# A recurrent attention with decay and a two-layer feed-forward: v*s as pieces of the output's column groups, two more stages with tiles from ScalarE and DMA transposes, and q~/k~ formed behind two sums

## The chip, the cores and the metric

The kernel runs on one core of one Trainium2 chip. The metric is the time of one execution on the device in microseconds; a kernel's time is the median of several runs. TensorE (PE) multiplies matrices from SBUF into PSUM, VectorE (DVE) and ScalarE (ACT) work elementwise, GpSimd (POOL) issues the loads and forms some tiles, and SyncE (SP) issues the stores and the DMA transposes.

## The reference

Two parts follow each other. The first is a linear attention with a decayed state, for 4 batches and 8 heads, 768 tokens of 48 channels:

```python
for t in range(S):
    cur = einsum('bhd,bhe->bhde', u[None] * k[t], v[t])
    y[t] = einsum('bhd,bhde->bhe', r[t], state + cur)
    state = w[None, :, :, None] * state + einsum('bhd,bhe->bhde', k[t], v[t])
```

The second takes y as 3072 rows of 384 channels: `h = x @ w_in` (384 to 2048), `g = max(0.01 h, h)`, `out = g @ w_out` (2048 to 384). Inputs and output are float32.

## The kernel before

**Stages.** The tokens are cut into 24 stages of 128 (6 for each batch, n = 0 to 23). Inside a stage the recurrence is written as matrix products: with q~ = r times a power of w and k~ = k times a power of w, a stage needs the products A = k~ q~ for each head, masked to the strict triangle; a state `st` carried from stage to stage; and the diagonal, whose entry s = sum over channels of r u k multiplies v. The output of a stage comes out transposed, channels on partitions, which is what the first product of the feed-forward takes as its moving operand.

**Steps of a stage**, with the letters that the written order uses: P (`prep`) forms q~ and k~ on DVE; T (`turn`) transposes them, eight TensorE matmuls against the identity and two evictions by ACT; A (`a_mm`) is the products into PSUM, M (`a_mask`) writes them masked to the tile `at` on DVE; X (`diag`) forms q~ times k~ on DVE for the diagonal; K (`kv_mm`) is k~ times v for the state, and S (`state`) decays it on DVE; Q (`prep2`) forms what the diagonal needs; Y (`y_part`) sums everything into the output and ACT copies it to `xT`.

**Two ways for the diagonal.** For stages below `DIAG` = 8, s comes out of TensorE as extra columns in K's bank (four matmuls against `wu`), Q forms `vs` = v*s on DVE, and Y ends with three whole 128x128 matmuls of `vs` against the identity. From stage 8 on, Q computes s on DVE (`ku`, `rku`, `s_tok`) and a tile of ident*s is laid into `at` ahead of the mask, which is then a predicated copy that leaves the diagonal: by POOL for stages 8 to 13 (two instructions for each stage), by ACT for later ones (eight for each stage). For stages below `TURNED` = 8, T transposes on TensorE; from 8 on, P forms q~ and k~ in one DVE instruction and SP issues one DMA transpose from `qk` to `tp`.

**Column groups.** Y writes 32 output channels at a time, in four column groups of the array that work side by side; each group gets its pieces (A's halves, and the state's) in rounds of four matmuls.

**Feed-forward.** G (`g1`) is the first product for one stage and four blocks of 128, J (`g1_pair`) that for two stages and two blocks; ACT applies the activation. H (`g2`) is the second product of a stage (16 matmuls of 128x384) and a copy and a store. For pairs 5 to 11 (`SEVEN`) the second product is done in seven half-size products instead of eight (`g2_seven`), with sums of operands on DVE (`g_sum`, `w_sum`) and sums of results, `plus`, on DVE.

**Order.** Every engine runs its instructions in the order in which the program records them; waits are set from reads and writes of named keys, and a read of a key that nobody has written yet sets no wait. The first stages and the feed-forward of the first three pairs are written out by hand in `ORDER`; L8 to L13 in it are the loads of stages 8 to 13, and the first loads are in `LOADS`, in their order. From pair m = 3 on a loop records, for each pair: the eight J products, the s of coming stages, sums, loads, A and M of stages 2m+4 and 2m+5, Y of 2m+2 and 2m+3, K and S, P of 2m+6 and 2m+7, and then the second product of pair m - 1. PSUM has eight banks, taken in rotation; at the end of each pair banks are skipped so that the rotation starts at the same place.

**Queues.** All loads of r, k, v and the weights are issued by POOL, in order; stores and DMA transposes by SP, in order. `w_out` comes as four slices, recorded from 3 down to 0, behind the loads of stages 1 to 7 and `w_in`.

## Time and profile before

| | before |
|---|---|
| median of 3 runs | 169.2 us (168.89 to 169.73) |
| profiled execution | 168.76 us, span 167.0 us, TensorE clock 1.0 throughout |
| PE busy | 160.9 us (96% of the span), 2275 matmuls |
| DVE busy | 120.7 us (72%) |
| ACT busy | 116.2 us (70%) |
| POOL busy | 82.2 us (49%) |
| DMA | 19.68 MB; DMA transposes of tp: 16, median 4.7 us from issue to landing |
| loads by POOL | r, k, v: 96 KB each, 4.9 to 5.5 us in the median; w_out: four of 384 KB, 10.4 us |
| mean duration of one | J matmul (128x256) 273 ns, H matmul (128x384) 326 ns, Y piece (32 columns) 224 ns, T matmul 254 ns; ACT tile of ident*s 388 ns; POOL half tile 1140 ns; predicated copy 1220 ns |

The span is the time from the first to the last instruction of the profiled execution; what the run takes on top of it, 1.76 us, is outside the trace. Matmuls are pipelined, so the duration of one is longer than the distance to the next: what a group costs TensorE is read from start to start. Rows by time give the start and duration in us, the engine, the line, the operation, the tiles and, in brackets, idle time ahead of it and what ended it.

### The profile page before, as it was taken

The numbers are of one execution on the slowest core, as the hardware profiler recorded it, in microseconds if no ns is written. First come the engines' busy times: TensorE is split into PE (matmuls) and PEld (weight loads), VectorE is DVE, ScalarE is ACT, GpSimd is POOL, SyncE is SP. The second block draws the span as 40 slices with busy tenths as digits, with TensorE's granted clock in tenths as the row PEclk, the third lists the DMA queues.
The fourth block names the chain that finished last, engine by engine and source line by source line (L and its number), as shares of the span: only waits on it lengthen the run. The fifth ranks groups of instructions, "written<-read, shape, count | busy, mean of one in ns | idle before, by whom it ended". The sixth has DMA issues, their size and how long they took to land.

```text
span 167.0 us, 5346 instructions
## 1 busy us (share of the span) xinstructions
PE 160.9 (96%) x2275; PEld 133.1 (80%) x2275; DVE 120.7 (72%) x232; ACT 116.2 (70%) x262; POOL 82.2 (49%) x97
## 2 busy tenths in 40 slices
PE   6799999999999999999999999999999999999994
PEld 1568898889656876876876889899897898898993
DVE  7699848751998959999279998799798267046253
ACT  4753898789112861989989889989899836828530
POOL 7999999991379797894840830910000000000000
PEclk9999999999999999999999999999999999999999
DMA  5999999999999989979997996999407102002022
GB/s 99 117 157 155 170 152 173 200 190 144 137 150 207 152 72 108 190 87 121 144 193 85 194 109 98 191 81 97 126 4 167 53 4 98 0 4 94 0 96 96
DMA packets 99260, 19.68 MB, mean 118 GB/s; under 512 B 92323, under 2 KB 99237, under 8 KB 99237
## 3 DMA queue, kind: packets, MB, share of 16 engines
q0 software_dynamic: 76512, 10.03, 92.5%
q1 hardware_dynamic: 21682, 9.11, 27.6%
q8 instruction: 18, 0.29, 0.7%
q10 hardware_dynamic: 1042, 0.20, 0.6%
q14 instruction: 6, 0.04, 0.1%
HBM read 20.45 MB, written 4.72 MB: 151 GB/s over the span
## 4 chain that ended last, share of the span: by engine, by line
PE 89%; POOL 4%; DVE 3%; ACT 1%; issue 1%; POOLq 0%
PE ps_all L566 31%; PE ps_all L647 18%; PE ps_all L583 16%; PE ps_all L549 7%; PE ps_all L516 5%; PE ps_all L399 4%; PE ps_all L375 3%; PE ps_all L433 2%; POOL rk_sb L218 2%; DVE at L409 1%; PE ps_all L521 1%; ACT tp L386 1%; DVE sum_t L486 1%; POOL v_sb L218 1%; DVE out_sb L678 1%
## 5 line engine op out<-in xcount | busy, mean ns | idle before, releaser
L566 PE MATMUL ps_all<-xT,w_in_sb 128*128 128x256 bf16 x480 | 54.5, 273 | 0.0
L566 PEld LDWEIGHTS ps_all<-xT,w_in_sb 128*128 128x128 bf16 x480 | 46.7, 98 | 5.8
L572 ACT ACTIVATE gT<-ps_all 128x512 bf16<-128x512 f32 x80 | 47.0, 596 | 4.9 <-PE ps_all L566 1.2
L218 POOL DMA_DIRECT2D rk_sb<-in_k_dram x23 | 21.5, 934 | 16.4 <-PE ps_all L566 16.4
L409 DVE CAST_PREDICATED at<-mask,ps_all 128x1024 bf16<-128x1024 uint16 x16 | 18.8, 1220 | 11.8 <-PE ps_all L399 11.7
L583 PE MATMUL ps_all<-w_out_sb,gT 128*128 128x384 bf16 x160 | 27.2, 326 | 0.0
L363 ACT ACTIVATE at<-ident,s_tok 128x128 bf16<-128x128 bf16 x80 | 24.8, 388 | 0.0
L583 PEld LDWEIGHTS ps_all<-w_out_sb,gT 128*128 128x128 bf16 x160 | 15.3, 98 | 9.7
L218 POOL DMA_DIRECT2D v_sb<-in_v_dram x24 | 22.5, 945 | 0.4 <-issue 0.4
L218 POOL DMA_DIRECT2D rk_sb<-in_r_dram x23 | 21.4, 930 | 0.0
L357 POOL TENSOR_TENSOR at<-ident,s_tok 128x512 bf16<-128x512 bf16 x12 | 13.4, 1140 | 9.7 <-DVE s_tok L347 9.7
L678 DVE TENSOR_TENSOR out_sb<-ps_all,snap 128x192 f32<-128x192 f32 x22 | 7.5, 356 | 12.9 <-PE ps_all L647 12.1
L647 PE MATMUL ps_all<-tw,gs 128*128 128x192 bf16 x168 | 16.0, 246 | 0.0
L589 ACT ACTIVATE out_sb<-ps_all 128x384 f32<-128x384 f32 x10 | 4.9, 487 | 14.6 <-PE ps_all L583 14.6
L536 ACT ACTIVATE xT<-ps_all 128x384 bf16<-128x384 f32 x24 | 11.0, 491 | 4.8 <-PE ps_all L516 3.0
L647 PEld LDWEIGHTS ps_all<-tw,gs 128*128 128x128 bf16 x168 | 14.0, 98 | 0.0
L549 PE MATMUL ps_all<-xT,w_in_sb 128*128 128x128 bf16 x192 | 12.8, 224 | 0.0
L549 PEld LDWEIGHTS ps_all<-xT,w_in_sb 128*128 128x128 bf16 x192 | 11.7, 101 | 0.5 <-DMA w_in_sb<-in_moe_w_in_dram 0.2
L554 ACT ACTIVATE gT<-ps_all 128x512 bf16<-128x512 f32 x16 | 9.6, 598 | 3.6 <-PE ps_all L549 2.9
L647 PE MATMUL ps_all<-w_out_sb,gT 128*128 128x192 bf16 x112 | 11.6, 246 | 0.2 <-ACT xT L536 0.2
L621 DVE TENSOR_TENSOR gs<-gT 128x1024 bf16<-128x1024 bf16 x14 | 9.6, 685 | 2.9 <-ACT gT L572 2.9
L417 DVE TENSOR_TENSOR at<-ps_all,mask 128x512 bf16<-128x512 f32 x16 | 10.3, 683 | 1.2 <-PE ps_all L399 1.2
(81 smaller groups left out, 234.1 us busy)
## 6 DMA issues: line engine op xcount, KB each, us to landing
out_dram<-out_sb SPq DMA_DIRECT2D x22, 192.0 KB, 3.1
v_sb<-in_v_dram POOLq DMA_DIRECT2D x24, 96.0 KB, 5.5
rk_sb<-in_r_dram POOLq DMA_DIRECT2D x23, 96.0 KB, 5.3
rk_sb<-in_k_dram POOLq DMA_DIRECT2D x23, 96.0 KB, 4.9
w_in_sb<-in_moe_w_in_dram POOLq DMA_DIRECT2D x4, 384.0 KB, 7.5
w_out_sb<-in_moe_w_out_dram POOLq DMA_DIRECT2D x4, 384.0 KB, 10.4
out_dram<-out_sb SPq DMA_DIRECT2D x4, 96.0 KB, 1.6
tp<-qk SPq DMA_TRANSPOSE x16, 4.7
```

The costliest lines, as they stand in the source:

```text
L218: add("pool", lambda: G.dma_start(dst, src), R=pace, W=[key], dma=f"{which}{n}")
L357: add("pool", lambda hh=hh, s_of=s_of: G.tensor_tensor(at[ia][:, hh, :, :], ident[:, :].unsqueeze(1).to_broadcast([128, NP, 128]), s_of.un ...
L363: add("act", lambda h=h: A.activation(at[ia][:, h % 2, h // 2, :], ident[:, :], AF.Copy, scale=s_tok[n % 2][:, h:h + 1]), R=["ident", ("s" ...
L409: add("dve", lambda: V.copy_predicated(at[n % NAT][:, :, :, :].rearrange("p two m i -> p (two m) i"), mask[:, :].bitcast(mybir.dt.uint16). ...
L417: add("dve", lambda hh=hh, part=part: V.tensor_tensor(at[n % NAT][:, hh, :, :], part, mask[:, :].unsqueeze(1).to_broadcast([128, NP, 128]) ...
L536: add("act", lambda: A.activation(xT[m % NX][:, :, 128 * half:128 * half + 128], ps_y[:, 0:HD].rearrange("p (s t) -> p s t", t=128), AF.Copy),
L549: last = PE.matmul(ps_g[:, 128 * f:128 * f + 128], w_in_sb[:, s, 128 * fb:128 * fb + 128], xT[ix][:, s, t], start=s == 0, stop=s == NSL - 1)
L554: add("act", lambda: A.activation(gT[ig][:, 4 * grp:4 * grp + 4, t], ps_g[:, :].rearrange("p (f t) -> p f t", t=128), AF.Prelu, alpha=0.01 ...
L566: last = PE.matmul(ps_g[:, 256 * f:256 * f + 256], w_in_sb[:, s, 128 * fb:128 * fb + 128], xT[ix][:, s, :], start=s == 0, stop=s == NSL - 1)
L572: add("act", lambda: A.activation(gT[ig][:, 2 * j:2 * j + 2, :].rearrange("p f t -> p (f t)"), ps_g[:, :], AF.Prelu, alpha=0.01), R=[key], ...
L583: last = PE.matmul(ps_o[:, 0:HD], gT[ig][:, s, 128 * half:128 * half + 128], w_out_sb[:, s, :], start=s == 0, stop=s == NFB - 1)
L647: done = PE.matmul(ps_o[:, 0:NH], lhs[:, s, :], rhs[:, s, :], start=first and s == 0, stop=s == HF - 1, skip_group_check=not (first and last))
```

## The change

- **v*s as pieces.** For stages that still use `vs`, Y no longer ends with three whole matmuls. Each 32-column block gets one more piece, `vs` against the identity, inside its column group, and each block starts and stops its own sum.
- **Stages 6 and 7.** `TURNED` and `DIAG` go from 8 to 6: stages 6 and 7 are transposed by DMA (two more DMA transposes, T6 and T7 are gone), their s is formed on DVE, their state adds on DVE, and their masks are predicated copies. Which stages POOL makes tiles for is now `POOLED` = 8 to 13, so the tiles of 6 and 7 are made by ACT, at the new step D. `ORDER` is rewritten from P5 on: A6, A7, M6 and M7 stand behind H1, A8, A9, M8 and M9 behind H3, and P9, Q9, P10 behind M7.
- **A pace for P.** `prep` takes a second argument, which adds a read of the key ("pace", 4, behind); `ORDER` uses it once, as P6.6.
- **q~/k~ ahead behind two sums.** In pairs whose second product is done in seven, P of the coming stages (18 to 23) is recorded inside `g2_seven`, behind the first two `plus`, and no longer ahead of it.
- **Banks.** The skip of banks at the end of a pair is left out for m = 10 as well, since no stages are ahead there.

```diff
-T4 Q3 G2.0 G2.1 G0.2 S3 G2.2 G1.2 Y3 P5 A4 P6 X4 M4 T5 X5 G3.0 K4 Q4 A5 S4 T6 G3.1 K5 G3.2 Y4 M5 L8 Q5 Y5 P7 A6 G1.3 J2.0 J2.1 T7
-M6 X6 X7 K6 J2.2 J2.3 A7 S6 J2.4 J2.5 L9 Q6 G2.3 G0.3 J2.6 M7 L10 J2.7 L11 G3.3 K7 S7 P8 Q7 Q8 P9 H0 Q9 K8 H1 P10 L12 K9 H2 S8 S9
-Y6 Y7 A8 A9 P11 M8 H3 M9 L13
+T4 Q3 G2.0 G2.1 G0.2 S3 G2.2 G1.2 Y3 P5 A4 X4 M4 T5 X5 G3.0 K4 Q4 A5 S4 G3.1 K5 G3.2 Y4 M5 L8 Q5 Y5 G1.3 J2.0 J2.1 J2.2 J2.3 J2.4
+J2.5 L9 Q6 P6.6 P7 G2.3 G0.3 J2.6 L10 J2.7 L11 G3.3 K6 S6 K7 S7 Q7 D6 D7 P8 Q8 H0 H1 A6 A7 M6 M7 P9 K8 Q9 P10 L12 H2 K9 S8 S9
+Y6 Y7 P11 H3 A8 A9 M8 M9 L13
...
-    TURNED, DIAG = 8, 8
-    LED = 14
+    TURNED, DIAG = 6, 6
+    POOLED = range(8, 14)
...
-    def prep(n):
+    def prep(n, behind=None):
         iq = n % NQK
+        pace = [] if behind is None else [("pace", 4, behind)]
...
-                R=[("r", n % NRK), ("k", n % NRK), "qtab", "ktab", ("qk0", iq)], W=[("qp", iq), ("kp", iq)])
+                R=[("r", n % NRK), ("k", n % NRK), "qtab", "ktab", ("qk0", iq)] + pace, W=[("qp", iq), ("kp", iq)])
...
-            if whole:
+            if whole and n in POOLED:
                 diag_tile(n)
...
+                if n < DIAG:
+                    one.append((vs[iv][:, 128 * s + 32 * q:128 * s + 32 * q + 32], ident[:, :]))
                 todo += [(s, a, m, i == 0, i == len(one) - 1) for i, (a, m) in enumerate(one)]
...
-                                         start=first_mm and (s == 0 or n >= DIAG),
-                                         stop=last_mm and n >= DIAG)
-            if n < DIAG:
-                for s in range(NSL):
-                    last = PE.matmul(ps_y[:, 128 * s:128 * s + 128], vs[iv][:, 128 * s:128 * s + 128], ident[:, :],
-                                     start=False, stop=s == NSL - 1)
+                                         start=first_mm, stop=last_mm)
...
             plus(2, 0, 0, 0)
             product(0, 2, 2, False, False)
             plus(0, 1, 1, 1)
+            for n in behind:
+                prep(n)
             product(1, 3, (low, two), False, True)
             plus(1, 2, 0, 1)
...
-        for n in (2 * m + 6, 2 * m + 7):
-            if n < NST:
+        coming = [n for n in (2 * m + 6, 2 * m + 7) if n < NST]
+        if m - 1 not in SEVEN:
+            for n in coming:
                 prep(n)
...
-        if m < NST // 2 - 1:
+        if ahead:
             while taken[0] % 8 != y_first:
                 taken[0] += 1
...
-            second(m - 1, tiles=[(n, h) for n in further for h in range(H)])
+            second(m - 1, tiles=[(n, h) for n in further for h in range(H)], behind=coming)
```

More of the change, by code (lines that the diff above doesn't have):

```diff
@@ L353, in diag_tile @@
         ia = n % NAT
-        if n < LED:
+        if n in POOLED:
             for hh in range(2):
@@ L621, in g_sum, with g2_seven @@
         add("dve", lambda: V.tensor_tensor(x[i][:, :, :], a, b, op), R=keys, W=[("gs", m % 2, i)])
-    def g2_seven(m, early=(), late=(), tiles=()):
+    def g2_seven(m, early=(), late=(), tiles=(), behind=()):
         ig, i2 = m % NG, m % 2
@@ L736, in u_table @@
         add("act", lambda: A.activation(u_tab[:, :], ps_u[:, 0:HD], AF.Copy), R=[key], W=["u_tab"])
-    steps = {"U": u_table, "P": prep, "Q": prep2, "T": turn, "A": a_mm, "M": a_mask, "K": kv_mm, "S": state, "Y": y_part, "X": diag, "C": decay_columns, "W": decay_table, "F": fill,
+    steps = {"U": u_table, "P": prep, "D": diag_tile, "Q": prep2, "T": turn, "A": a_mm, "M": a_mask, "K": kv_mm, "S": state, "Y": y_part, "X": diag, "C": decay_columns, "W": decay_table, "F": fill,
              "G": g1, "J": g1_pair, "H": g2, "L": lambda n: load_stage(n, pace=[("pace", (n - 4) // 2, (n - 4) % 2)])}
@@ L741, in bass_rwkv5_eagle__then__act_leaky_relu_kernel, with second @@
         steps[name[0]](*(int(x) for x in name[1:].split(".") if x))
-    def second(m, early=(), late=(), tiles=()):
+    def second(m, early=(), late=(), tiles=(), behind=()):
         if m in SEVEN:
-            g2_seven(m, early, late, tiles)
+            g2_seven(m, early, late, tiles, behind)
         else:
@@ L752, in bass_rwkv5_eagle__then__act_leaky_relu_kernel @@
         ahead = [n for n in (2 * m + 4, 2 * m + 5) if n < NST]
-        further = [n for n in (2 * m + 6, 2 * m + 7) if LED <= n < NST]
+        further = [n for n in (2 * m + 6, 2 * m + 7) if n not in POOLED and n < NST]
         for j in range(8):
@@ L756, in bass_rwkv5_eagle__then__act_leaky_relu_kernel @@
         for n in ahead:
-            if n < LED:
+            if n in POOLED:
                 prep2(n)
```

## The prediction

> **What bounds the kernel now.** I read the page first, then the answers by time (PE, DVE, SP, POOL), then the landings of single transfers. The page:

> ```profile
> PE 160.9 (96%) x2275; PEld 133.1 (80%) x2275; DVE 120.7 (72%) x232; ACT 116.2 (70%) x262; POOL 82.2 (49%) x97
> DMA  5999999999999989979997996999407102002022
> PE 89%; POOL 4%; DVE 3%; ACT 1%; issue 1%; POOLq 0%
> ```

> TensorE is busy 96% of the span, so every matmul removed is worth its time unless something else is late there. DMA row: the engines are full until about 75 us, and the change puts new transfers into that stretch. So I read the stretch row by row (start, duration, ...):

> ```profile
> 41.52 2.76 PE L583 MATMUL ps_all<-w_out_sb,gT 128*128 128x384 bf16 x16
> 42.84 4.08 SPq L318 DMA_TRANSPOSE tp<-qk  x2
> 60.15 2.35 DVE L409 CAST_PREDICATED at<-mask,ps_all 128x1024 bf16<-128x1024 uint16 x2 [1.78 <-PE ps_all L399]
> 76.82 1.02 DVE L316 TENSOR_TENSOR qk<-rk_sb,tab 128x768 bf16<-128x768 bf16 x2
> 77.40 4.03 SPq L318 DMA_TRANSPOSE tp<-qk  x2
> 84.25 0.67 PE L399 MATMUL ps_all<-tp 48*128 48x128 bf16 x16
> ```

> H0 (first GEMM-2 product) starts at 41.52. DVE runs without a gap from M10 at 60.15 to P14/P15 at 76.82. The transposes of 14 and 15 follow at once, the second from about 78.7. How long it takes is in the issues of 78.70 to 78.75 us:

> ```profile
> tp<-qk SPq DMA_TRANSPOSE x1, 5.7
> ```

> 78.7 + 5.7 = 84.4, and A14/A15 start at 84.25: A15's operand is there 0.1 us before it is used (its 16 matmuls take 0.67 where the same group elsewhere takes 0.62). The chain of waits shows PE here, but DVE and the transposes stand just as close to the end. In the first 85 us PE time saved is worth something only if that chain moves too.

> **The change, part by part.**

> *PE work removed ahead of H0.* Start to start in the PE rows: T6 0.46, T7 0.45; the two s columns of K6 and K7 0.10 each; the carried state of K7 0.17: 1.28 us. A6 and A7 (0.33 each) only move behind H1. *Pieces:* a round of four column-group matmuls starts every 0.057 us (15.54, 15.60, 15.66, ...). Three more rounds are 0.17; the three whole matmuls they replace take 0.18 from start to start, so each of Y0 to Y5 gains 0 to 0.08, together 0.1. [...] *A part of T6 is lost:* Y5 needs v*s of stage 5, which DVE forms at 30.16 to 30.71, and DVE is late there for reasons that stay. PE would reach Y5 at 30.35 and waits to 30.7. So H0 is reached at 41.52 - 1.28 - 0.66 - 0.1 + 0.35 = 39.8.

> *New transposes of stages 6 and 7.* On DVE q~/k~ of 6 follow s of 6 (0.39 + 0.39 + 0.47, from 30.7) and end at 32.4; SP issues at 32.5. The token P6.6 should pace it, but the order listing of the changed kernel shows no wait at that row, because J2.6 is recorded later; instead J2.6 waits for P6, five microseconds early, which costs nothing. So both transposes enter while the output weights are landing. Weight slice 0, the last, is issued at 27.0:

> ```profile
> w_out_sb<-in_moe_w_out_dram POOLq DMA_DIRECT2D x2, 384.0 KB, 11.6
> ```

> This is the median of slices 1 and 0 (11.0 and 12.2): slice 0 lands at 39.2, 2.3 us before H0 now, and 0.6 us before the H0 of the changed kernel. What do two transposes cost the loads beside them? Alone, 2112 packets (two transposes) pass in about 2.5 us (125 to 131 us). Beside loads, the trace shows it once: from 44.3 on about 1.45 transposes are served until stage 11's v lands at 49.4, where the 0.7 us spacing of its neighbours puts it at 47.6: 1.8 us late for 1.8 us of service, one for one. Bounds for slice 0: 0 (room left) and 2.5 us (both served first); I take 2.3, near the upper end, since the pair of 42.84 was through within 8.2 us, which is 40.7 for a pair issued at 32.5. So H0 starts at 41.5, as now, and the 1.7 us won are gone. [...]

> *Behind H0* (A6 at t = H0 + 5.2 = 46.7). M6 starts at t+0.5, M6 and M7 take 2.3, so P9, now behind them, ends at t+3.3. K9 reads it: PE is there at 0.55 + 0.17 + 2.6 = t+3.3, no wait, but nothing spare. Behind K9 stand Y6, Y7 and H3, which need no more than M7. Y6/Y7 without their whole matmuls save 0.64 (1.39 to 0.75). A9 is reached at t+7.1 and needs the transpose issued at t+3.4. Landings are 3.2 with no loads beside them (the pairs from 89 and 125) and 4.1 to 6.7 with loads; I take 5.0, between the 4.1 issued at 48.23 and the 5.4 before it: a stall of 1.3, bounds 0 and 3.0.

> *POOL.* s of stage 9 comes behind P9, at t+4.6 (47.7 now). Its tile (2.3) ends at t+6.9, the six loads behind it on POOL (5.3, as 50.17 to 55.45 now) at t+12.2, the tiles of 10 and 11 (2.1 each) at t+16.4. M11 needs the last: 63.1, where it starts at 61.28 now. From there DVE has no gap, so P14 and P15, their transposes and A15 all come 1.8 us later: A15 at 86.3 for 84.5. PE's own way there is shorter (t+7.1+1.3, then 30.5: the 33.1 us from A9 to A15 now, less H3, which moves ahead: 85.6), so the stall at A9 is covered by this one. A first loss that stays hidden behind a second is the reason why I do not add them.

> *ACT.* Sixteen tiles of 0.30 pitch (4.8 us) replace four evictions of tp (2.1). ACT has 2.88 of 10 us busy from 40 to 50; s of 7 ends at 42.4 (K6 and K7 do not wait for weights; then S6, S7 and 1.25 for Q7), its eight tiles at 44.9, and M7 needs them at t+1.6 = 48.3. H0's store copy behind them waits 0.8 us; its bank is next used by K9, 5 us later. Without that cover M7 would move by what ACT is late. *DVE:* ku, rku and s of two stages 2.5 us and half a microsecond for the state of 7, less prod 0.7, v*s 0.9 and the masks' and q~/k~'s difference 0.3: +1.1, inside its gaps between 32 and 42.

> *P behind two sums (stages 18 to 23).* Both sums come 1 us earlier, so two PE holes go: 0.41 at 126.2 (product waits for a sum) and, through the banks that are not skipped for m = 10, 0.21 at 145.1. P18 moves from 100.0 to 102.0; its pair's second transpose goes out at 103.9 and lands at 3.6 later, 107.5, A19 being at 108.5. For 20 and 21: 115.7 + 4.4 = 120.1 against 120.3. Loads of 22 and 23 (issued from 104.1) run beside the first pair, so 0 to 1 us; I take 0.1. Sum -0.5.

> **Sum.** +1.8 - 0.5 = +1.3 us on the profiled execution of 168.76 (span 167.0 and 1.76 around it): 170.1. The median of the runs is 169.2, 0.44 above the profiled one: 170.5.

> **Rivals.**
> - *Room in the DMA rows (faster).* The engines serve transposes beside loads for nothing, as pairs with no loads beside them land in 3.2. Then slice 0 still lands at 39.2, H0 is at 39.8, t = 45.0, A9 does not stall, and the later gate goes too (A15's operand comes 2.5 us sooner than 5.7). PE alone decides: A15 at t+37.6 = 82.6, -1.9, later -0.5: 166.8 by the median. It decides if slice 0 is under 0.6 late. Against it: the one-for-one delay at 49.4.
> [...]
> - *A9 is the gate.* The transpose behind P9 takes 6.7, as the one issued at 50.93 did: stall 3.0, A15 at 46.7 + 7.1 + 3.0 + 30.5 = 87.3, +2.8 - 0.5: 171.5. For it: the loads are still landing; against it: 4.1 at 48.23.

> **How the numbers follow.** My forecast 0.43 (its own range 170.0 to 170.7, from slice 0 being 1.8 to 2.5 late), room 0.21, tile chain 0.18, A9 0.18. Range: 166.8, the faster case, to 171.7, the A9 case with slice 0 at its bound. Within 0.5% (0.85 us, about what a measurement here can tell from no change) are the tile-chain case and the lowest fifth of mine: 0.26. Slower 0.53, faster 0.21.

> **What would show it.** Right: H0 after 41.0 with PE waiting for w_out's transfer ahead of it, A9 waiting for a transpose, POOL's tiles of 11 ending after 62, A15 at 85.8 or later; no hole at 126 and 145. Wrong: H0 at 39.8 with no wait, transposes of 6 and 7 through in 4 us with the loads unmoved, A15 before 84.

## The result and the profile after

The changed kernel takes 175.64 us in the median (174.57 to 176.09, 4 runs) against 169.29 us for the kernel before in the same comparison: a ratio of 1.0365, 95% interval 1.0311 to 1.042. It is slower, by 6.35 us, and above the upper end of the predicted range. Here and below, a run of a kernel that lies more than 1.5% above its fastest one is not in its ratio. The profiled execution took 175.5 us with a span of 173.8. From its page:

```profile
PE 162.9 (94%) x2298; PEld 134.4 (77%) x2298; DVE 119.0 (68%) x231; ACT 118.4 (68%) x274; POOL 81.9 (47%) x97
PEclk9999999999999699999999999978999999999999
DMA  6999999999999999939996991993620801102022
PE 61%; DMA 17%; POOL 16%; DVE 3%; issue 1%; DVEq 0%; POOLq 0%
```

Two things are new. The chain of waits no longer is TensorE (61% for 89%): loads and the DMAs themselves hold a third of it. And the granted clock, full in the kernel before as far as its trace records it (from 15.24 us on), has two dents, at about 57 and 117 us. TensorE's rows by time show what stands ahead of each:

```profile
40.20 5.36 PE L581 MATMUL ps_all<-w_out_sb,gT 128*128 128x384 bf16 x32
49.75 0.33 PE L434 MATMUL ps_all<-v_sb,qk 128*128 128x96 bf16 x4 [0.76 <-DVE qk L317]
56.30 0.40 PE L400 MATMUL ps_all<-tp 48*128 48x128 bf16 x8 [2.46 <-DMA tp<-qk]
114.37 0.40 PE L400 MATMUL ps_all<-tp 48*128 48x128 bf16 x8 [1.80 <-DMA tp<-qk]
117.64 2.05 PE L645 MATMUL ps_all<-tw,gs 128*128 128x192 bf16 x16
```

H0 starts at 40.20 without a wait. K9 waits 0.76 us for P9, A9 2.46 us for its transpose, A19 1.80 us for its own. The last row, sixteen half-size products, took 1.32 us from start to start elsewhere and takes 1.89 here: it runs in the second dent. Granted clock by stretch (start:end and its length; then busy time and instructions of each engine; then PEclk, DMA share, GB/s):

```profile
54.00:57.00 3.00, 0.70 (x12) 0.59 (x13) 1.72 (x3) 0.04 (x1) 3.00 (x5) 1.00 1.39 178
57.00:61.00 4.00, 4.00 (x24) 2.96 (x22) 3.86 (x7) 1.79 (x3) 3.24 (x4) 0.57 1.83 177
111.00:115.00 4.00, 2.20 (x51) 1.65 (x51) 2.92 (x6) 1.76 (x3) 2.32 (x3) 1.00 2.90 124
115.00:119.00 4.00, 4.00 (x74) 3.67 (x63) 2.51 (x4) 2.18 (x6) 0.00 (x0) 0.57 1.62 126
```

After each wait TensorE has 3.41 us at half clock (in the trace's clock records 57.36 to 60.77 and 115.39 to 118.80), which costs 1.7 us. The loss in order of time: J3, the first product of pair 3, starts 2.34 us later than before (56.64 for 54.30), A10 4.0 us later (63.65 for 59.64), A18 still 4.0, J8 7.5 (122.23 for 114.70), and 0.8 comes back behind it, where the two holes at 126 and 145 are gone. The clock is not the larger part of the loss: one of the four runs has a mean granted clock of 1.0, so no such window, and it took 174.57 us.

Where the transposes of 6 and 7 went (SyncE's queue, then VectorE):

```profile
32.69 14.19 SPq L319 DMA_TRANSPOSE tp<-qk  x3
49.63 5.14 SPq L319 DMA_TRANSPOSE tp<-qk  x2
106.75 2.62 SPq L319 DMA_TRANSPOSE tp<-qk  x2
```

```profile
45.00 0.56 DVE L317 TENSOR_TENSOR qk<-rk_sb,tab 128x768 bf16<-128x768 bf16 x1 [2.14 <-DMA rk_sb<-in_r_dram]
46.79 2.35 DVE L410 CAST_PREDICATED at<-mask,ps_all 128x1024 bf16<-128x1024 uint16 x2
49.05 0.55 DVE L317 TENSOR_TENSOR qk<-rk_sb,tab 128x768 bf16<-128x768 bf16 x1
```

They were issued at 32.7 and their packets moved from 36.7 to 44.0. P8 (45.00) waits 2.14 us for r of stage 8; M6 and M7 follow, and P9 behind them at 49.05. The DMA queues in the stretch from 38 to 44 us (queue, packets, MB, share of 16 engines), first before, then after; q0 carries the loads, q1 the transposes:

```profile
q0 software_dynamic: 8779, 0.84, 264.4%
```

```profile
q1 hardware_dynamic: 1684, 0.42, 101.0%
q0 software_dynamic: 1846, 0.20, 75.9%
```

6,933 packets of loads are missing, at the pace of before (1,463 a us) 4.7 us of loading. The 1,684 packets that took their place would pass in an estimated 2.2 us with nothing beside them: two transposes alone, 2,112 packets, took 2.8 (the kernel before, 90.56 to 93.33). The loads of stages 8 to 11 pay for it: r of 11 lands 17.3 us after its issue for 10.8, v of 11 18.3 for 12.1.

The packets show two things inside this stretch. First, loads and transposes advance packet for packet: 760 of the one and 763 of the other from 37.25 to 39.75 us (in `e3_no_sums`, from 37 to 44 us, 1,964 and 1,968), so that the loads go no faster than the transposes, 304 a us for 1,463. Second, from 41.75 to 42.75 both nearly stop, with 29 and 28 packets. What the engines moved from 38 to 44 us, in slices of 0.15 us, shows it; the second line is the same stretch of `e5_whole`, a kernel of the experiments below with the same two transposes:

```profile
GB/s 156 164 136 108 101 102 98 81 101 90 85 76 108 132 149 153 151 260 147 112 102 150 146 144 39 12 9 13 7 9 9 9 11 149 157 152 159 156 146 127
```

```profile
GB/s 152 122 75 34 155 159 154 144 78 98 85 88 63 79 138 150 135 153 150 152 157 153 77 151 156 156 157 153 158 153 155 159 130 126 139 142 143 140 139 136
```

The stop begins 1.0 us after the queue that carries instructions (q8) has moved 16 KB, at 40.67. The other five traces with these transposes and such a move among them (`e3_no_sums`, `e4_fill`, `e6_fetch`, `e8_p9`, `e10_spare`) have such a stop 1.0 to 1.2 us after it (`e10_spare` has a second one that no such move explains); `e5_whole`, whose moves come at 35.44 and 44.16, has none, and there the pair passes in 6.4 us for 7.4. So the move is the likely cause of the stop; no run moves it away from these two transposes and changes nothing else.

### The profile page after: what moved, and what is told of

Read it like the earlier page. It is cut to its first block, busy times and chain, and to the rows that moved or that the text cites. A ratio compares the mean times of both kernels' runs of the same rounds, so it can differ in the third digit from the quotient of the medians.

```text
span 173.8 us, 5415 instructions
## 1 busy us (share of the span) xinstructions
PE 162.9 (94%) x2298; PEld 134.4 (77%) x2298; DVE 119.0 (68%) x231; ACT 118.4 (68%) x274; POOL 81.9 (47%) x97
## 4 chain that ended last, share of the span: by engine, by line
PE 61%; DMA 17%; POOL 16%; DVE 3%; issue 1%; DVEq 0%; POOLq 0%
PE ps_all L564 25%; PE ps_all L645 19%; DMA rk_sb<-in_r_dram 9%; PE ps_all L581 9%; POOL rk_sb L218 8%; DMA tp<-qk 7%; POOL v_sb L218 4%; PE ps_all L519 4%; PE ps_all L400 2%; POOL w_out_sb L232 2%; POOL w_in_sb L228 2%; PE ps_all L434 2%; DVE qk L317 1%; DVE at L410 1%; DVE out_sb L676 1%
## 5 line engine op out<-in xcount | busy, mean ns | idle before, releaser
L564 PE MATMUL ps_all<-xT,w_in_sb 128*128 128x256 bf16 x480 | 55.9, 278 | 0.0
L570 ACT ACTIVATE gT<-ps_all 128x512 bf16<-128x512 f32 x80 | 46.7, 595 | 9.4 <-PE ps_all L564 5.8
L564 PEld LDWEIGHTS ps_all<-xT,w_in_sb 128*128 128x128 bf16 x480 | 47.5, 100 | 6.5
L364 ACT ACTIVATE at<-ident,s_tok 128x128 bf16<-128x128 bf16 x96 | 29.6, 389 | 0.0
L218 POOL DMA_DIRECT2D rk_sb<-in_k_dram x23 | 21.5, 933 | 16.4 <-PE ps_all L564 16.4
L410 DVE CAST_PREDICATED at<-mask,ps_all 128x1024 bf16<-128x1024 uint16 x18 | 21.3, 1219 | 11.4 <-PE ps_all L400 11.4
L676 DVE TENSOR_TENSOR out_sb<-ps_all,snap 128x192 f32<-128x192 f32 x22 | 7.8, 356 | 16.4 <-PE ps_all L645 15.8
L645 PE MATMUL ps_all<-tw,gs 128*128 128x192 bf16 x168 | 16.6, 251 | 0.0
L645 PEld LDWEIGHTS ps_all<-tw,gs 128*128 128x128 bf16 x168 | 14.6, 100 | 0.1
L400 PE MATMUL ps_all<-tp 48*128 48x128 bf16 x192 | 9.0, 228 | 4.5 <-DMA tp<-qk 4.3
L519 PE MATMUL ps_all<-at,v_sb 128*32 128x128 bf16 x384 | 12.1, 229 | 0.4 <-DVE vs L339 0.4
L645 PE MATMUL ps_all<-w_out_sb,gT 128*128 128x192 bf16 x112 | 12.2, 255 | 0.0
L547 PEld LDWEIGHTS ps_all<-xT,w_in_sb 128*128 128x128 bf16 x192 | 11.7, 101 | 0.6 <-issue 0.2
L400 PEld LDWEIGHTS ps_all<-tp 48*128 48x128 bf16 x192 | 5.8, 98 | 8.0 <-issue 3.9
## 6 DMA issues: line engine op xcount, KB each, us to landing
w_in_sb<-in_moe_w_in_dram POOLq DMA_DIRECT2D x4, 384.0 KB, 6.9
w_out_sb<-in_moe_w_out_dram POOLq DMA_DIRECT2D x4, 384.0 KB, 10.4
```

What stands on the lines that cost most here:

```text
L218: add("pool", lambda: G.dma_start(dst, src), R=pace, W=[key], dma=f"{which}{n}")
L364: add("act", lambda h=h: A.activation(at[ia][:, h % 2, h // 2, :], ident[:, :], AF.Copy, scale=s_tok[n % 2][:, h:h + 1]), R=["ident", ("s" ...
L400: last = PE.matmul(at_bank[n][hh][0][:, 128 * p:128 * p + 128], tp[it][rows, NP + p, :], tp[it][rows, p, :], start=True, stop=True)
L410: add("dve", lambda: V.copy_predicated(at[n % NAT][:, :, :, :].rearrange("p two m i -> p (two m) i"), mask[:, :].bitcast(mybir.dt.uint16). ...
L519: last = PE.matmul(ps_y[32 * q:32 * q + 32, 128 * s:128 * s + 128], a, m, start=first_mm, stop=last_mm)
L547: last = PE.matmul(ps_g[:, 128 * f:128 * f + 128], w_in_sb[:, s, 128 * fb:128 * fb + 128], xT[ix][:, s, t], start=s == 0, stop=s == NSL - 1)
```

## The experiments

The theory after this profile: (a) two more transposes in the full stretch hold up the loads far beyond their own time, P8 and the transpose behind P9 come late, A9 waits; (b) P18 and P19 behind two sums bring a transpose among the loads of 22 and 23, A19 waits; (c) each wait is followed by half clock. Rivals: the pieces are dear on TensorE, the new order (P9 behind M6 and M7) is the loss, or the clock falls for reasons of its own.

**The pieces alone** (`e1_pieces`):

```diff
+                if n < DIAG:
+                    one.append((vs[iv][:, 128 * s + 32 * q:128 * s + 32 * q + 32], ident[:, :]))
...
-            if n < DIAG:
-                for s in range(NSL):
-                    last = PE.matmul(ps_y[:, 128 * s:128 * s + 128], vs[iv][:, 128 * s:128 * s + 128], ident[:, :],
```

> The kernel before, with v*s as pieces of the column groups and nothing else of the change. Theory (the loss comes from the transposes: two new ones among the loads, and those of 18 and 19 issued later): the pieces are no part of it; H0 0.1 us earlier, Y6 and Y7 together 0.6 us shorter, and 168.7 to 169.3 us in all, since the chain over DVE and the transpose of stage 15 holds A15 at 84.3. [...]

Measured 169.47 us, a ratio of 1.0038 (1.0012 to 1.0063). The first rival, that the pieces are dear on TensorE, has little room in 0.4%: they are no part of the 6.35 us to speak of; but no gain either: the 0.4% lies just above the range that I gave. One row of its trace holds more than that:

```profile
35.72 0.22 PE L433 MATMUL ps_all<-v_sb,qk 128*128 128x96 bf16 x1 [0.90 <-issue]
```

The last of K6's four matmuls starts 0.90 us late and waits for nothing that the profile shows. Up to J2.0 TensorE is where it was in the kernel before (32.67 for 32.68), behind this row it is 1.06 us late, and 0.69 us at the end. The traces of `e6_fetch` (1.16 us at 33.97) and `e7_turn` (1.00 us at 31.38) have such a stop too. Counted in recorded matmuls and weight loads, the stops stand behind number 1,203, 1,203 and 947, and 1,203 less 947 is 256. The likely cause is TensorE's own instructions coming late (more on their moves below), not the pieces; that is argued, and no run tests it.

**The sums alone** (`e2_sums`):

```diff
+            for n in behind:
+                prep(n)
             product(1, 3, (low, two), False, True)
```

> The kernel before, with q~/k~ of stages 18 to 23 formed behind two sums and nothing else of the change (the banks at the end are as before). Theory: the second transpose of the pair 18 and 19 meets the loads of 22 and 23, takes 6 us instead of about 4, A19 waits 1.5 to 2 us, and the TensorE clock falls to 0.5 for 3.4 us right behind it (1.65 us more); the hole at 126.2 is gone (-0.4): 171.5 to 172.3 us. Rival (A19's wait in the changed kernel only comes of the delays before it): A19 waits under 0.3 us and the run takes 168.6 to 169.2.

Measured 169.26 us, 1.0006 (0.9972 to 1.0041): the rival's side. A19 waits 0.32 us, by the profile for ScalarE:

```profile
110.32 0.40 PE L399 MATMUL ps_all<-tp 48*128 48x128 bf16 x8 [0.32 <-ACT gT L572]
```

So (b) as I had it falls: the step loses nothing on its own in sum. It gains nothing either: against the kernel before, TensorE is 1.39 us late at A18, 1.87 at A19 and 1.36 at J9 (128.23 for 126.87), behind the place of the hole at 126, so that what A19 loses comes back there. The loads of 22 and 23 stand in the same place there: POOL issues the first of them 1.46 us after SyncE's pair, in the changed kernel 1.31. The pair's second transpose lands 6.1 us after the pair was issued (4.9 us after its own), 0.14 us before A19 starts; in the changed kernel after 7.5. There A9 and A19 start 0.13 us behind the landing of theirs, so the transpose may have ended the 0.32 us as well as ScalarE. The step had used up the slack, and something else then took 1.3 us more.

**The changed kernel without the sums** (`e3_no_sums`): P of the coming stages ahead of the second product again.

> The changed kernel with q~/k~ of all stages ahead of the second product, as before. Theory: the 4.0 us lost up to A10 stay, A19 no longer waits and no clock dip follows it, the holes at 126 and 145 come back in part: 172.0 to 172.7 us. Rival (as above): the wait at A19 stays, 175 to 176 us.

Measured 172.62 us, 1.0211 (1.0176 to 1.0246), as the theory had it: in company the sums cost 1.5%, 2.6 us (3.0 by the medians), although alone they cost nothing. The difference is A19's: at A18 both kernels are 4.0 us behind the kernel before. They get there differently, and that the theory's 4.0 us came out is in part luck: here A10 is only 2.78 us late, and the rest is a wait of 1.12 us for the transpose of stage 13. One thing I had not expected:

```profile
56.74 0.40 PE L400 MATMUL ps_all<-tp 48*128 48x128 bf16 x8 [2.74 <-DMA tp<-qk]
```

```profile
PEclk9999999999999999999999999999999999999999
```

A9 waits even longer than in the changed kernel, and no half clock follows. So (c) needs a condition; it is below.

**Something to do during the waits** (`e4_fill`):

```diff
+        if n in WARM:            # WARM = {9: 9, 19: 7}
+            def warm():
+                for _ in range(WARM[n]):
+                    last = PE.matmul(at_bank[n][0][0][:, :], ones[:, 0:128], ones[:, :], start=True, stop=True)
+                return last
```

> The changed kernel with idle products of ones (128x512, nine of them ahead of A9 and seven ahead of A19) into the bank that A9 or A19 then overwrites: TensorE has something to do while A9 and A19 wait for their transposes. They wait as long as in the changed kernel (their transposes land no sooner). Theory (the half clock behind both waits comes of the idle time): granted clock 0.95 or more in 57 to 61 and 115 to 119 us, A10 1.7 us and the end 3.3 us earlier than in the changed kernel, 172.0 to 172.7 us. Rival (the clock falls for another reason, or the products cost as much as the clock): the dips stay, 175 to 176.5 us.

Measured 173.3 us, 1.0252 (1.0196 to 1.0307): 1.1% or 1.9 us less than the changed kernel (2.3 by the medians), of 3.3 expected. The same stretches as above:

```profile
57.00:61.00 4.00, 4.00 (x40) 3.04 (x39) 2.75 (x7) 1.94 (x4) 3.72 (x5) 1.00 1.67 177
115.00:119.00 4.00, 4.00 (x102) 3.87 (x99) 2.64 (x4) 3.24 (x11) 0.00 (x0) 1.00 1.87 139
```

Both dents are gone although A9 and A19 come no sooner relative to their transposes (they start 0.61 and 0.23 us behind the landing, for 0.13). This trace alone does not settle it: without the products TensorE would have stood idle some 1.5 us ahead of each, less than what brings half clock by the cases below. All four runs together say more: three have a mean granted clock of 0.999 or 1.0, and one of four in the changed kernel. That idle TensorE brings the half clock rests on these and on the cases below. The profiled run has another dent, from 41.27 to 44.68: TensorE stood 2.00 us ahead of H0, from 39.2 on, until the last packets of w_out were in (40.77; the profile names ScalarE there, whose work was done). That is the wait of my prediction, in a kernel where I had not meant to make it.

**The condition.** The clock records step by 3.413 us, in all the traces that have them (all but that of `e1_pieces`). With these windows laid over TensorE's waits, a window is followed by half clock where TensorE stood idle 1.71, 1.80, 2.00, 2.35, 2.41 or 3.41 us inside it (six cases, in `e7_turn`, the changed kernel, `e4_fill`, the changed kernel, `e8_p9`, `e5_whole`), and not where it stood 1.68 (`e10_spare`, 42.11 to 45.52 us), 1.44, 1.39, 1.35, 1.19 or less. The border lies about half a window. It is no sharper than some hundredths: the 1.71 us of `e7_turn` are 1.77 if weight loads are not counted as work, and 1.73 us behind the last matmul of `e8_p9` bring no half clock. The 2.74 us of `e3_no_sums` fall across two windows, 1.35 and 1.39. Where a window begins relative to the kernel differs from run to run (the first full one starts at 13.96 to 17.77 us in these traces), so a wait of 2 us costs 2 or an estimated 3.7 us by chance.

**What else met the transposes of 18 and 19.** In the trace's packets, queue q8 moves 16 KB of instructions at 110.42 us in the changed kernel, while the second transpose is on its way, and packets of 256 and 96 bytes take up to 1.5 us each right behind. It does so 17 or 18 times in a run; TensorE's 2 x 2298 instructions are 18 times 256, so it is estimated to be one move for every 256 of them. In `e2_sums` the move came at 113.0, behind the pair. Three runs move it. First, `e5_whole`, the changed kernel with whole products of v*s (54 matmuls fewer):

> The changed kernel with the three whole products of v*s in Y0 to Y5, as before, instead of pieces: 54 matmuls fewer on TensorE, about the same TensorE time. In the changed kernel queue q8 moves 16 KB of instructions at 110.42 us, while the second transpose of 18 and 19 is under way, and packets of the transposes take up to 1.5 us around it; with the sums alone (no pieces) such a move fell at 113.0 and A19 did not wait. Theory (the move of instructions among the transposes makes A19 late; it comes every 256 instructions of TensorE): with 108 instructions fewer it falls behind A19, A19 waits under 0.4 us with no half clock behind it: 171.8 to 172.8 us. Rival (the loads of 22 and 23 make A19 late): the wait of 1.8 us and the run's 175 to 176 us stay.

Measured 174.74 us, 1.0274 (1.0199 to 1.035): missed, but not for A19.

```profile
114.46 0.40 PE L400 MATMUL ps_all<-tp 48*128 48x128 bf16 x8 [0.88 <-DMA tp<-qk]
```

The move fell at 105.3 and 118.1, ahead of and behind the pair; the pair's packets take 3.9 us for 4.7, A19 waits 0.88 for 1.80, and no half clock follows. So by this comparison about half of the wait was the move of instructions; the other half stays without it. The loads beside the pair are its likely cause (3.9 us, where pairs with no loads take 2.8 to 3.1), which no run shows. The total missed because A9 waited 4.04 us in this run, with half clock behind it. Then `e6_fetch`, idle products ahead of stage 0:

```diff
+            for _ in range(SMALL if n == 1 else 0):    # SMALL = 40
+                last = PE.matmul(ps[i][:, 0:16], ones[:, 0:128], ones[:, 0:16], start=True, stop=True)
```

> The changed kernel with 40 idle products of 128x16 ones ahead of stage 0, most of them in the 1.0 us in which TensorE waits for the identity there (at most 0.8 us longer in all): 80 more instructions of TensorE, so the 16 KB of instructions of 110.4 us are moved about 4 us sooner, at 106 to 107, as the first transpose of the pair begins. Theory (instructions among the transposes): A19 waits under 0.5 us, 172.0 to 173.2 us. Rival (the loads of 22 and 23): A19 waits 1.8 us as in the changed kernel, 175.5 to 176.5 us.

Measured 175.25 us, 1.0305 (1.0269 to 1.0342). Inconclusive: the move came at 107.6, when the pair had been issued (107.2), not ahead of it, and A19 waits 2.04 us. The clean test is the same edit in the kernel before, with 34 products (`e9_shift`), where nothing else differs:

> The kernel before with 34 idle products of 128x16 ones ahead of stage 0, where TensorE waits for the identity: 68 more instructions of TensorE and nothing else. In the trace of before, queue q8 moves 16 KB of instructions at 79.6 and at 116.0 us, inside the pairs of transposes whose packets run from 78.7 to 82.9 (4.2 us) and from 114.1 to 118.2 (4.0 us); pairs with no such move inside and no loads take 2.8. Theory (a move of instructions among the transposes costs them 1.1 us or more): the moves come some 3 us sooner, ahead of both pairs, which then take 2.7 to 3.2 us each; a pair that a move now meets takes 3.9 or more. The time stays within 0.8 us of before, as TensorE does not wait for these pairs. Rival (the pairs are slow there for other reasons): both still take 4.0 or more.

Measured 170.01 us, 1.0029 (1.0002 to 1.0056). The pair of 14 and 15 and that of 20 and 21 in the DMA issues, before and then in `e9_shift` (q8: moves, MB, share; tp: issues in the stretch, median us to landing):

```profile
q8 instruction: 1, 0.02, 3.9%
tp<-qk SPq DMA_TRANSPOSE x1, 5.7
...
q8 instruction: 1, 0.02, 3.0%
tp<-qk SPq DMA_TRANSPOSE x1, 4.4
```

```profile
tp<-qk SPq DMA_TRANSPOSE x1, 3.8
...
tp<-qk SPq DMA_TRANSPOSE x2, 3.2
```

With the moves at 76.6 and 113.3, ahead of both pairs, their packets take 3.2 and 2.8 us for 4.2 and 4.0; the pair of 12 and 13, which now meets one at 68.2, takes 6.1 for 5.0. A move of instructions among transposes costs them 1.0 to 1.2 us: shown.

**The transposes of 6 and 7 taken out** (`e7_turn`): without the sums, T6 and T7 on TensorE behind J2.6 and J2.7, all else as changed.

```diff
-    TURNED, DIAG = 6, 6
+    TURNED, DIAG = 8, 6
```

> The changed kernel with q~/k~ ahead of the second product as before, and stages 6 and 7 transposed on TensorE again (T6 behind J2.6, T7 behind J2.7; their tiles from ScalarE stay). Theory (the two new transposes hold up the loads, so that the loads and the transpose behind P9 come late): loads of 8 to 11 land 4 to 6 us sooner, the transpose behind P9 takes 4 to 5 us for 6.5, A9 waits under 0.8 us for 2.7: 169.8 to 171.0 us. Rival (P9's new place behind M6 and M7 is what makes A9 late): P9 still ends at 49, its transpose takes 6 or more, A9 waits 1.5 us or more: 171.8 to 173 us.

The six runs without a half-clock window give 1.0073 (1.0033 to 1.0113). With the four that have one (172.45 to 174.18 us, mean granted clock 0.98 to 0.99) the median is 171.38 us, 1.0107 of the kernel before; the trace is of one of these four. r of 11 lands as follows (issue to landing):

```profile
rk_sb<-in_r_dram POOLq DMA_DIRECT2D x1, 96.0 KB, 11.8
```

11.8 us for 17.3, the transpose behind P9 lands after 3.1 us for 6.5, and A9 does not wait, though P9 still starts at 49.71. The theory holds: against `e3_no_sums` the two transposes cost 1.4%, 2.3 us by the ratios, and 1.0%, 1.8 us, if all ten runs count here. What remains against before, 1.2 us by the ratio, is the rest of the change: order, tiles and pieces. One part of it is in VectorE's rows, and in this trace a larger one in TensorE's:

```profile
64.30 1.22 DVE L410 CAST_PREDICATED at<-mask,ps_all 128x1024 bf16<-128x1024 uint16 x1 [1.03 <-POOL at L358]
```

```profile
61.73 0.40 PE L400 MATMUL ps_all<-tp 48*128 48x128 bf16 x8 [1.01 <-DMA tp<-qk]
76.02 0.40 PE L400 MATMUL ps_all<-tp 48*128 48x128 bf16 x8 [1.71 <-DMA tp<-qk]
```

M11 waits for POOL's tile: the gate of my prediction, seen once the larger waits are gone. A11 and A13 wait for their transposes, which take 6.9 and 7.7 us among the loads of stages 12 to 15, and half clock follows the second wait.

**P9 ahead of M6 and M7** (`e8_p9`), without the sums, the transposes kept:

```diff
-... H0 H1 A6 A7 M6 M7 P9 K8 ...
+... H0 H1 A6 A7 P9 M6 M7 K8 ...
```

> The changed kernel with q~/k~ ahead of the second product as before, and P9 recorded ahead of M6 and M7 instead of behind them; the new transposes stay. Theory (loads): r and k of stage 9 land at 47, so P9 can start 1.5 us sooner at most, and its transpose still takes 6 us or more among the late loads: A9 waits 1.2 to 2.2 us for 2.7, 171.6 to 172.6 us. Rival (the place of P9): A9 waits under 0.5 us, 169.8 to 170.6 us.

Measured 174.09 us, 1.0248 (1.0192 to 1.0304).

```profile
46.52 1.30 DVE L317 TENSOR_TENSOR qk<-rk_sb,tab 128x768 bf16<-128x768 bf16 x1 [0.24 <-DMA rk_sb<-in_r_dram]
```

```profile
56.78 0.40 PE L400 MATMUL ps_all<-tp 48*128 48x128 bf16 x8 [3.03 <-DMA tp<-qk]
```

P9 starts 2.7 us sooner than in `e3_no_sums`, as soon as r of 9 is there, and ends 1.9 us sooner, as it takes 1.30 us for 0.55. A9 starts when it did: the transpose issued at 47.84 takes as much longer as it starts earlier, in the queue of late loads. The place of P9 is not the cause. (The time is above both expectations; half clock follows A9 here, 1.7 us that neither of them had.)

**The two transposes alone, in the kernel before** (`e10_spare`), behind P7, into tiles that are overwritten unread:

> The kernel before with two DMA transposes more, issued behind P7 into tiles that stage 8 and 9 overwrite later and nobody reads; nothing else is changed, so the order on TensorE, VectorE and ScalarE is that of before. Theory (the transposes hold up the loads beside them, and that is the first loss of the changed kernel): loads of stages 8 to 11 land 3 to 6 us later than before, the transposes of 9 or 10 come late, A8 to A11 wait 1.5 us or more in all: 171 to 173 us. Rival (the new order of the steps is the loss; the transposes alone are covered): the loads land up to 2.5 us late and A8 to A11 wait under 0.5 us, 168.8 to 169.8 us.

Measured 174.83 us, 1.0284 (1.022 to 1.0348), above the theory's range. TensorE's waits (us in total, times, longest), without those for `ones` and the identity that the changed kernel has too:

```profile
PE ps_all L589 <- DMA w_out_sb<-in_moe_w_out_dram: 2.5, 1, 2.5
PE ps_all L435 <- DMA v_sb<-in_v_dram: 1.9, 1, 1.9
...
PE ps_all L405 <- DMA tp<-qk: 1.4, 1, 1.4
```

5.8 us of waits from two transposes that nobody needs, with the old order of every other engine. They are issued sooner here (25.9 and 31.4), so that they hold up v of 7 and the output weights as well; r of 11 lands after 20.1 us. No version among these beats the kernel before.

## Why the prediction was wrong

The direction was right, the size not: +1.3 us predicted on the profiled execution, +6.7 measured on it. Of the two terms of the sum, +1.8 up to A15 measured +4.0 (88.49 for 84.51), and -0.5 behind it measured +2.8.

- *H0 reached at 39.8:* right, 40.20, with the first record of a full clock 1.2 us later than before (16.40 for 15.24).
- *Slice 0 of w_out 2.3 us late:* wrong here. Its last packet came at 39.72 for 38.93, 0.8 late, and H0 did not wait. In other kernels with the same transposes slice 0 landed from 0.1 us sooner (`e8_p9`) to 3.1 later (`e6_fetch`) than before, and without them 1.3 later in `e7_turn`, so one trace does not tell the transposes' share.
- *One for one:* **the step that failed.** I had taken 1.8 us of delay for 1.8 us of service from the one place where the trace showed both. In the full stretch it was 4.7 us of loads for an estimated 2.2 us of transposes, and I charged it to the weights, when most of it fell on the twelve loads behind them. One for one holds for packets there and not for time, and some 1.0 us of the 4.7 is the stop that follows a move of instructions.
- *P9 at t + 3.3, K9 with no wait:* P9 ended at 49.60, A6 (t) was at 45.49: t + 4.1, as P8 waited for r of 8. K9 waited 0.76.
- *A9's stall of 1.3 (0 to 3.0):* 2.46. The transpose took 6.5 us, near the 6.7 of the bound, the row that I had argued against. This was the rival "A9 is the gate", priced at 171.5.
- *POOL's tile chain as the gate:* the tile of stage 11 ended at 63.6, near the 63.1 worked out, but M10 started at 64.16, after A9. It ended a wait only in `e7_turn`. That it holds alone, the case with a chance of 0.18, asked for transposes that take less of the engines than one for one; how much less was my estimate, which no run shows. In the changed kernel slice 0 was 0.8 us late, and the loads lost 4.7 us to an estimated 2.2 us of transposes.
- *The clock:* not in the sum at all. The profile of before shows it full, and I priced waits as if it would stay so: in the profiled run it cost 1.7 us behind A9 and 1.65 behind A19.
- *The sums, -0.5 us:* the two holes went, as said. The second transpose was given 3.6 us, landing at 107.5, one us ahead of A19; alone it landed just in time (`e2_sums`), in the changed kernel A19 waited 1.80, by the comparison with `e5_whole` about half of it by a move of instructions that the changed count of TensorE's instructions had put there (0.88 without it).
- *Pieces 0.1 us of gain, ScalarE nothing:* no gain (+0.4%, e1); no wait for ScalarE's tiles decided anything in the changed kernel. Narrow weights are no dearer to load by the trace of before: loads of 32 and of 128 columns take 98 ns alike (L516 and L566).
- *P6.6 sets no wait:* right; SyncE issued at 32.69, for the 32.5 worked out without one.

By the ratios, the 3.65% are: order, tiles and pieces 0.73 (`e7_turn`, 1.2 us), the two transposes 1.38 (`e3_no_sums` against it, 2.3 us), the sums in their company 1.54 (2.6 us). With all ten runs of `e7_turn` the first two are 1.07 and 1.04, so the split between them is rough.

## What to carry to other kernels

A transpose put among loads that fill the DMA engines is to be charged with more than its own time (by the estimates 2.1 times in the changed kernel; 1.5 in `e5_whole`, where no move of instructions fell among it and 3.7 us of loads went for 2.4), and to the loads that are queued behind it, not to itself. A step that is moved up to the slack of its consumer can cost nothing alone and 2.6 us in company, as the sums did: give the slack as a number, and ask what could take it. A wait of TensorE of more than some 1.7 us can cost nearly twice its length (A19 in the changed kernel: 1.80 us, and 1.65 in the half clock behind it), so that filling it with idle products is worth trying (1.9 us less in `e4_fill`) even where the wait itself cannot be removed.
